# Attention with a feed-forward layer: another order of the first two chunks, with fixed buffer rooms

## The chip, the core and the metric

The kernel runs on one core of one Trainium2 chip. TensorE (PE in the rows) multiplies matrices, VectorE (DVE), ScalarE (ACT) and GpSimd (POOL) work on vectors, and SyncE (SP) issues the DMAs. Each engine takes its instructions strictly in the order of the program and waits on semaphores for the others. The metric is the device time of one execution in microseconds (us).

## What is computed

Local attention with block summaries over 4 batches, 8 heads, 768 positions and 64 features a head, and then a two-layer feed-forward network on its output. Everything is float32.

```python
k_sum = k.reshape(B, H, nb, block, D).max(axis=3)      # 24 blocks of 32
v_sum = v.reshape(B, H, nb, block, D).mean(axis=3)
scores_l = where(|i - j| < 16, scale * q @ k.T, -1e9)   # scale 1/8
scores_s = scale * q @ k_sum.T + log(32)
a = softmax(concat([scores_l, scores_s]))
x = a @ concat([v, v_sum])                              # 3072 x 512
h = maximum(x @ w_in, 0)                                # 512 -> 2048
out = (h * h) @ w_out                                   # 2048 -> 512
```

## The kernel before

**Tiling.** Of the 3072 rows, 128 make a group (24 groups, 6 a batch) and two groups a chunk of 256 (12 chunks). The 2048 hidden features are 16 tiles of 128. A weight arrives as the words of a float64 and is made on the chip into a high and a low float32r half; each product of the feed-forward layers is then three matmuls (high times high, low times high, high times low). One feature tile of a chunk costs 12 matmuls of 256 columns in the first layer (`ffn1`, L382) and 6 of 512 columns, some of them halved, in the second (`ffn2`, L429).

**Two parts.** The chunks 2 to 11 run in a regular loop (`slot`, `period`) that the change does not touch. The first two chunks (groups 0 to 3), the whole preparation of the weights, and the attention of groups 4 to 7 are written out by hand in one string, `START` (L43). Each of its tokens is one step, and the steps are emitted in the order of the string, so the string sets the order on each engine. The framework adds the waits for the data and for buffers that are used again. The tokens are:

- `L:..` a load on SP: `q`, `k`, `v` of a group, `kv` and `kw` (transposed keys of batch 0, keys and values of batch 1, a head pair each), `w` (the words of a feature tile: `w2.1` the half for the first layer, `w2.2` for the second, `w4` both), `vn` (values of batch 0), `mask` (constants).
- `KS` block maxima of a pair's keys (DVE, L180); `S4.0` half the scores of group 4 (PE, L285 for groups 0 to 3, L269 later); `TT0.3` mask and maximum of group 0, head 3 (DVE, L297); `E0.3` its exponential (ACT, L305); `NR` and `N` reciprocal sums (DVE, L318) and the normalisation (POOL, L325) of four heads.
- `T` a transposition on PE (L331) and `TC` its copy out of PSUM (L126). `SV` block means of the values on PE (L149) and `VC` four copies of them, two instructions each, into the two value buffers. `O` the attention output (PE, L352), `XH` and `XL` its high and low half (ACT L366, DVE L369).
- `HI`, `LO`, `SH`, `AD`, `CA`, `SU` the six steps that make a weight (ACT; ACT or DVE; DVE; POOL; ACT or DVE; DVE or POOL).
- `F1.u.j` and `F2.u.j` first and second layer of unit `u`, a pair of feature tiles of chunk 0 or 1; `RE`, `SQ`, `MU`, `GL` the square of its result. `Z15` fifteen matmuls of zeros that fill PE. `XT` one small exponential. A letter `a`, `v` or `p` behind a token names the engine; digits behind `=` name PSUM banks.

**Buffers.** Weights, raw words and key/value tiles share one pool of 18 buffers of 8 KB a partition (`room`, L209), given out in turn. A load waits until the buffer's last use is over, and DMAs wait in SP's queue in order. At most eight DMAs of SP are under way, since eight semaphores are used in turn.

Of the kernel before, what the change touches and what calls it, by code (L numbers as in the profile page):

```python
# [40 lines left out]


START = """  # L43
Z15 XT L:q0 L:kv0 L:kv1 KS0 L:kv3 KS1 L:kv2 KS3 S0.0=01 Z6 L:mask KS2 TT0.3 S0.1=23 TT0.1 L:q1 TT0.0 L:w0.1 L:w1.1
TT0.2 S1.0=45 L:q2 TT0.6 E0.3 TT0.4 E0.1 L:w2.1 TT0.7 S1.1=45 Z5 E0.0 E0.6 PK4v E0.2 NR0.0 TT1.7 TT1.0 TT1.2 E0.4
HI0.1 E1.7 L:q3 TT1.5 TT1.1 TT1.3 E1.2 LO0.1v N0.0p SH0.1 T0.0=0 Z2 HI1.1 E1.1 TT0.5 TT1.6 E1.3 S2.1=12 SH1.1 LO1.1v
S2.0=12 E1.0 TC0.0v TT1.4 E0.7 NR1.0 TT2.0 E1.5 TT2.3 E0.5 S3.1=30 AD1.1 S3.0=30 E1.4 E1.6 NR1.1 N1.0p HI2.1 E2.3
CA1.1v TT2.1 N1.1p E2.0 CA0.1a T1.0=4 Z2 NR0.1 TT3.2 TT3.0 L:vn0 L:vn1 L:q4 T1.1=5 Z1 TT3.1 TC1.0v L:k4 E3.1 N0.1p
E3.2 SU1.1p L:v1 T0.1=4 TT3.4 TT3.7 TT3.6 SV Z1 TT3.5 E3.0 TT3.3 TC1.1a E3.3 AD0.1 E2.1 TT2.7 SU0.1p TT2.4 L:v0 TT2.5
TC0.1a TT2.2 E2.7 E3.6 S4.1=03 TT2.6 NR3.0 N3.0p E2.2 S4.0=03 L:w3.1 VC1v E2.5 E3.4 E2.6 E3.5 VC0v VC3v L:w0.2 VC2v  # L50
NR2.0 L:w1.2 PK5v SH2.1 E2.4 E3.7 O1=5 N2.0p NR2.1 O0=1 XH1 XH0 HI3.1 NR3.1 XL1 T2.0=2 N3.1p LO2.1a T3.0=4 CA2.1a XL0
TT4.2 HI0.2 TC3.0v TT4.0 L:v3 T3.1=5 LO3.1a TC2.0v N2.1p TC3.1a AD2.1 LO0.2v F1.0.0=1 L:v2 T2.1=4 TC2.1a F1.0.1 O3=2
O2=5 SH3.1 CA3.1a HI1.2 SH0.2 SU2.1v XH3 L:w2.2 L:w3.2 AD3.1 CA0.2a L:q5 RE0v XH2 LO2.2a F1.1.0=4 SU3.1v SH1.2 F1.1.1
HI3.2 HI2.2 SQ0 L:w4 XL3 RE1a TT4.6 AD0.2 L:w6 LO1.2v XL2 SH2.2 L:k5 F1.2.0=2 SH3.2 MU0 LO3.2a MU1 AD1.2 TT4.7
F1.3.0=5 L:w5 GL0v SU0.2v F1.2.1 CA1.2a L:kw0 HI4 SQ1 LO4a L:w8 L:w7 SH4 F2.0.0 L:w10 CA2.2v SU1.2v CA3.2a AD2.2
SU2.2v AD3.2 RE2v TT4.4 GL1v HI6 TT4.1 F1.3.1 F2.0.1 CA4a TT4.5 L:w12 S5.1=14 SU3.2p S5.0=14 MU2 F2.1.0 E4.4 LO6a RE3v
AD4 HI5 SQ2 F2.1.1 SH6 TT4.3 SU4v E4.2 SH5 EV0.1a SQ3 F1.4.0=0 AD6 CA6a MU3 L:w9 L:w11 F1.6.0=3 GL2v EV0.0v SU6v TT5.0
TT5.1 LO5a F2.2.0 GL3v TT5.5 HI8 F1.5.0=2 CA5a F2.2.1 HI7 AD5 TT5.4 LO7v SU5v F1.7.0=5 SH8 LO8a SH7 HI10 TT5.2 F1.4.1
L:kw1 RE4v TT5.3 TT5.7 CA7a MU4 SH10 AD7 F1.6.1 LO10a E4.7 L:q7 SU7v F2.3.0 F2.3.1 SQ4 CA8a GL4v F1.5.1 HI12 AD8 RE6v
RE5v AD10 F2.4.0 MU5 F2.4.1 SQ5 CA10a HI9 F1.7.1 SH12 GL5v SU8p LO12a TT5.6 MU6 RE7a CA12a SH9 L:w13 SU10v SQ6 LO9a  # L60
VT1 AD12 F2.5.0 MU7 SU12v F2.5.1 L:w14 EV1.0a L:q6 SQ7 EV1.1v GL6v F1.8.0=0 KT1 CA9a HI13 F1.13.0=2 L:w15 L:k7 GL7p
KT0 F1.12.0=1 AD9 F1.10.0=4 E4.5 L:v5 LO13v SU9v HI11 F2.6.0 E5.7 F2.6.1 SH13 SH11 F1.9.0=5 E4.1 VT0 E4.3 E5.1 E4.0
F1.8.1 L:k6 CA13a E5.6 F2.7.0 CA11a E5.4 HI14 AD13 LO11v SU13v RE8v SQ8 E5.0 L:v4 AD11 NR4.0 E5.5 F2.7.1 MU8 SU11v
F1.14.0=3 E4.6 SH14 F1.10.1 CA14a GL8v E5.3 RE10a F1.12.1 NR5.1 F1.9.1 N4.0p LO14v F1.13.1 RE9v AD14 F2.8.0 F1.14.1
NR4.1 SQ9 MU9 F2.8.1 MU10 HI15 GL9v F2.9.0 LO15a SQ10 SH15 SU14v N4.1p AD15 E5.2 F1.11.0=0 TU4.1 F2.9.1 GL10v CA15a
TU4.2 TU4.0 RE12v F2.10.0 SU15p L:kw2 KT2 F1.11.1 RE11a NR5.0 L:kw3 SQ11 F1.15.0=5 MU11 GL11v RE13a F2.10.1 N5.1v KT3
F2.11.0 SQ12 MU12 N5.0p MU13 F2.11.1 PK6a GL12p F1.15.1 SQ13 EV2.1v S6.1=01 S6.0=01 O4=4 EV2.0v PK7a F2.12.0 F2.12.1
GL13p TU5.0 F2.13.0 RE14a TU5.2 XH4 SQ14 MU14 RE15a F2.13.1 GL14p TU5.1 VT2 S7.0=23 XL4 SQ15 S7.1=23 F2.14.0 MU15
GL15v O5=4 VT3 F2.14.1 XH5 XL5
"""  # L70


# [1 line left out]
def attn_ffn_kernel(ctx: ExitStack, tc: tile.TileContext, q, k, kt, v, vt, v0, w, consts, out):  # L74
    nc = tc.nc
# [63 lines left out]
    def load_v(g):  # L139
        nc.sync.dma_start(out=v_sb[g % 2][0:96], in_=v[g // NT, g % NT])  # L140

    def sum_v0(vn):
# [10 lines left out]
        return ps
# [583 lines left out]
```

## Time and profile before

| what | before |
|---|---|
| median of 3 runs | 606.64 us (606.45 to 610.62) |
| the profiled execution | 607.6 us, its span 605.8 us |
| TensorE busy | 593.8 us, 98% of the span |
| VectorE, ScalarE, GpSimd busy | 386.0, 265.8, 105.2 us |
| TensorE clock granted | 0.999 on the mean, that is the 2.4 GHz level |
| last wait of TensorE for another engine or a DMA of the kernel | 36.7 us after the span's start |

The span runs from the first instruction to the last. The 1.8 us between it and the execution's time lie around it. The share of busy time is a mean over two very different parts, so stretches of it are shown further down.

### The profile page before, as it was taken

The page shows a single profiled execution, that of the slowest core. Times are in us where ns is not written, and L with a number is a line of the kernel's source. Part 1 is how long each engine was busy: PE and PEld are TensorE (multiplying, and loading weights), DVE is VectorE, ACT ScalarE, POOL GpSimd, SP SyncE. Part 2 cuts the span into 40 slices and gives each one's busy share as a digit, 9 for nine tenths or more (in the row PEclk, how much of TensorE's full clock was granted, in tenths as well). Part 3 has the DMA queues.
Part 4 walks back from the last instruction along what each step waited for, and adds up shares of the span by engine and source line. Part 5 has one row for each costly group of instructions (what it writes and reads, how often), then busy time and mean ns, then how long its engine had stood idle before and what let it go on. Part 6 is the DMA issues. An engine that isn't in the chain of part 4 may idle for free.

```text
span 605.8 us, 14834 instructions
## 1 busy us (share of the span) xinstructions
PE 593.8 (98%) x6178; PEld 572.8 (95%) x6178; DVE 386.0 (64%) x1063; ACT 265.8 (44%) x687; POOL 105.2 (17%) x97
## 2 busy tenths in 40 slices
...
GB/s 274 328 363 417 204 260 56 112 168 35 1 11 269 2 2 226 2 2 226 2 1 199 81 2 131 97 2 87 88 2 38 139 2 2 88 1 2 36 1 35
DMA packets 19890, 60.46 MB, mean 100 GB/s; under 512 B 2288, under 2 KB 2288, under 8 KB 18288
## 3 DMA queue, kind: packets, MB, share of 16 engines
...
## 4 chain that ended last, share of the span: by engine, by line
PE 95%; DMA 3%; DVE 1%; ACT 0%; issue 0%; SPq 0%
PE o_ps L429 43%; PE ph L382 39%; PE s_ps L382 4%; PE ph L352 4%; PE s_ps L269 3%; DMA v_sb<-in_v 1%; DMA q_sb<-in_q 1%; DMA kv<-in_kt 1%; DVE v_sb L126 1%; PE s_ps L285 0%; PE o_ps L149 0%; PE o_ps L563 0%; PE ph L331 0%; PE ph L285 0%; PE s_ps L352 0%
## 5 line engine op out<-in xcount | busy, mean ns | idle before, releaser
L382 PE MATMUL ph<-xh,w_sb 128*128 128x256 f32 x1376 | 241.2, 278 | 0.5 <-DVE xl L369 0.5
L429 PE MATMUL o_ps<-w_sb,gh 128*128 128x256 f32 (+1 forms) x1428 | 237.5, 285 | 0.0
L382 PEld LDWEIGHTS ph<-xh,w_sb 128*128 128x128 f32 x1376 | 213.3, 188 | 8.7 <-issue 1.3
L429 PEld LDWEIGHTS o_ps<-w_sb,gh 128*128 128x128 f32 x1428 | 191.0, 188 | 0.5 <-issue 0.3
L382 PE MATMUL ph<-xl,w_sb 128*128 128x256 f32 x688 | 190.5, 277 | 0.0
L429 PE MATMUL o_ps<-w_sb,gl 128*128 128x256 f32 (+1 forms) x670 | 150.5, 294 | 0.0
L401 DVE TENSOR_TENSOR ph<-ph,r 128x512 f32<-128x512 f32 x85 | 59.3, 699 | 141.5 <-ACT r L390 140.7
L390 ACT ACTIVATE r<-ph 128x512 f32<-128x512 f32 x84 | 49.9, 594 | 189.3 <-PE ph L382 189.3
L382 PEld LDWEIGHTS ph<-xl,w_sb 128*128 128x128 f32 x688 | 129.2, 188 | 0.0
L338 DVE STREAM_TRANSPOSE pT<-e_sb 32x256 f32<-32x256 f32 x240 | 104.6, 436 | 4.1 <-POOL e_sb L325 0.7
L305 ACT ACTIVATE e_sb<-e_sb,nmx 128x120 f32<-128x120 f32 x192 | 73.7, 386 | 75.5 <-DVE nmx L297 75.5
L429 PEld LDWEIGHTS o_ps<-w_sb,gl 128*128 128x128 f32 x670 | 104.6, 188 | 0.4
L325 POOL TENSOR_TENSOR e_sb<-e_sb,total 128x480 f32<-128x480 f32 x47 | 46.2, 991 | 322.1 <-DVE total L319 150.4
L396 ACT ACTIVATE gh<-r 128x512 fp32r<-128x512 f32 x94 | 59.5, 633 | 12.1 <-PE o_ps L429 6.5
L404 DVE TENSOR_TENSOR gl<-ph,gh 128x512 fp32r<-128x512 f32 x85 | 58.8, 692 | 9.2 <-DVE ph L401 0.5
L297 DVE CUSTOM_DVE_ANT_0 e_sb<-s_ps,consts_sb 128x120 f32<-128x120 f32 x180 | 40.7, 277 | 1.9 <-PE ph L331 1.1
L245 POOL TENSOR_TENSOR w_raw<-w_raw 128x1024 int32<-128x1024 int32 (+1 forms) x20 | 35.9, 1800 | 24.7 <-DVE w_raw L234 8.6
L305 ACT ACTIVATION_READ_ACCUMULATOR e_sb<-e_sb,nmx 128x1 f32 x192 | 36.3, 189 | 0.0
L369 DVE TENSOR_TENSOR xl<-ph,xh 128x512 fp32r<-128x512 f32 x22 | 15.2, 691 | 23.3 <-ACT xh L366 23.2
L382 PE MATMUL s_ps<-xh,w_sb 128*128 128x256 f32 x160 | 28.6, 279 | 0.0
L366 ACT CAST xh<-ph 128x512 fp32r<-128x512 f32 x22 | 12.9, 586 | 33.1 <-PE ph L352 33.1
L352 PEld LDWEIGHTS ph<-pT,v_sb 128*64 128x64 f32 x704 | 21.7, 138 | 5.2 <-issue 3.8
...
## 6 DMA issues: line engine op xcount, KB each, us to landing
...
```

The source lines that it names most:

```text
L245: nc.gpsimd.tensor_tensor(out=lo, in0=hi, in1=lo, op=ALU.add)
L297: nc.vector.tensor_tensor_reduce(out=e_sb(g)[:, h, 0:NK], in0=s_ps[g, half][h % 2][:, h // 2, 0:NK], in1=m, scale=-scale, scalar=3.0e38, o ...
L305: nc.scalar.activation(e, e, AF.Exp, bias=nmx[g, half][:, i : i + 1], scale=-1.0, accum_out=sm[g, half][:, i, 0:1])
L325: eng.tensor_mul(out=e, in0=e, in1=sm.pop((g, half)).unsqueeze(2).to_broadcast([P, 4, NK]))
L338: nc.vector.transpose(out=pT[g % 2][j * 32 : j * 32 + 32, :, i * 32 : i * 32 + 32], in_=e_sb(g)[i * 32 : i * 32 + 32, :, j * 32 : j * 32 + ...
L352: nc.tensor.matmul(xp[o : o + 64, h // 2, s * 64 : s * 64 + 64], lhsT=v_sb[g % 2][:, s, h * 64 : h * 64 + 64], rhs=pT[g % 2][:, h, s * 64 ...
L382: nc.tensor.matmul(ph, lhsT=w_sb[f][:, w, cc * P : (cc + 1) * P], rhs=x[c][:, cc, :], start=(n == 0), stop=(n == 3 * NC4 - 1))
L390: nc.scalar.activation(r, ph, AF.Relu)
L396: nc.scalar.activation(gh, r, AF.Square)
L401: nc.vector.tensor_mul(out=ph, in0=ph, in1=r)
L404: nc.vector.tensor_sub(out=gl, in0=ph, in1=gh.bitcast(F32))
L429: nc.tensor.matmul(o_ps[c][tt][:, o : o + step], lhsT=g_[:, ts_], rhs=w_sb[f][:, w, DM + o : DM + o + step], start=start and o == 0, stop= ...
```

## The change

The string `START` is written anew: 508 tokens for 506, nearly the same steps in another order, some of them on another engine. The buffers of the pool are no longer given out in turn; each tile has a fixed room, from tables. The load of the constants is split in two (the masks that the first groups use, and the rest), and the block means of the values are split in two halves. The loop behind the string is the same, instruction for instruction. Line numbers behind the tables are 2 to 4 higher after the change.

```diff
 SPARE = 2
+RAW_ROOM = (5, 3, 2, 10, 12, 14, 15, 16, 8, 3, 5, 0, 8, 14, 3, 0)
+W_ROOM = (7, 9, 4, 11, 13, 1, 17, 10, 2, 15, 16, 6, 12, 8, 5, 14)
+KV0_ROOM, VN_ROOM, KV_FIRST, KV_ROOM = (0, 1), (6, 8), (3, 12, 5, 6), (0, 3)
...
-Z15 XT L:q0 L:kv0 L:kv1 KS0 L:kv3 KS1 L:kv2 KS3 S0.0=01 Z6 L:mask KS2 TT0.3 S0.1=23 TT0.1 L:q1 TT0.0 L:w0.1 L:w1.1
...
+L:kv1 KS1 L:q0 L:kv0 Z15 KS0 S0.0=01 L:mask TT0.1 TT0.0 TT0.2 E0.2 TT0.3 E0.3 L:q1 S1.0=45 E0.0 TT1.1 E1.1 TT1.0 E1.0
+Z6 L:kv2 KS2 L:kv3 KS3 L:w2.1 E0.1 S0.1=23 S1.1=45 TT0.5 TT1.2 HI2.1 E0.5 LO2.1v NR0.0 N0.0p E1.2 L:rest TT1.5 TT1.3
...
-    def sum_v0(vn):
...
-        ps = ps_o.tile([P, DM], F32, name="o_ps")
-        for t in range(NT):
+    def sum_v0(vn, n, ps):
+        if n == 0:
+            ps = ps_o.tile([P, DM], F32, name="o_ps")
+        for t in range(n * NT // 2, (n + 1) * NT // 2):
...
-    def room(dtype, name):
...
-        return big.tile([P, 8192 // mybir.dt.size(dtype)], dtype, name=name, tag="w", bufs=NF + SPARE)
+    def room(dtype, name, n):
...
+        return big.tile([P, 8192 // mybir.dt.size(dtype)], dtype, name=name, tag=f"room{n}")
...
-            w_raw[f] = room(I64, "w_raw")
+            w_raw[f] = room(I64, "w_raw", RAW_ROOM[f])
...
-            nc.sync.dma_start(out=consts_sb, in_=consts)
+            nc.sync.dma_start(out=consts_sb[:, 0 : 2 * NK], in_=consts[:, 0 : 2 * NK])
+        elif what == "rest":
+            nc.sync.dma_start(out=consts_sb[:, 2 * NK :], in_=consts[:, 2 * NK :])
...
-            v_mean[0] = sum_v0([vn[0], vn[1]])
+            v_mean[0] = sum_v0(vn, i, v_mean.get(0))
```

Three places of the order follow. Numbers behind `e_sb`, `pT` and `v_sb` tell apart the buffers of even and odd groups.

ScalarE, the start of the program before, with the semaphores that each row waits for: `XT` (`junk`) comes first, then exponentials of group 0.

```order
L640 ACT_TABLE_LOAD
L640 ACTIVATE junk<-zero_90 128x1 [waits DVE_49]
L305 ACTIVATE e_sb_77,sm<-e_sb_77,nmx 128x120 [waits DVE_49] x4
L305 ACTIVATE e_sb_77,sm<-e_sb_77,nmx 128x120
L305 ACTIVATE e_sb_77,sm<-e_sb_77,nmx 128x120 [waits DVE_49]
```

And ScalarE, the same place after the change:

```order
L307 ACT_TABLE_LOAD [waits DVE_49]
L307 ACTIVATE e_sb_77,sm<-e_sb_77,nmx 128x120 [waits Pool_49]
L307 ACTIVATE e_sb_77,sm<-e_sb_77,nmx 128x120 [waits DVE_49]
L307 ACTIVATE e_sb_77,sm<-e_sb_77,nmx 128x120
L307 ACTIVATE e_sb_78,sm<-e_sb_78,nmx 128x120 [waits DVE_49] x2
```

`XT` has moved to some 100 rows further down, and the table load now stands behind the first exponential's wait for VectorE.

ScalarE, after the change, around the output of groups 0 and 1. Before, the eight copies into `v_sb` stood on VectorE, and all 32 exponentials of groups 0 to 3 stood ahead of the first `xh`.

```order
L129 CAST w_sb<-w_raw 128x512
L307 ACTIVATE e_sb_78,sm<-e_sb_78,nmx 128x120 x2
L129 COPY v_sb_73<-o_ps 32x2x128
L129 COPY v_sb_74<-o_ps 32x2x128
L129 COPY v_sb_73<-o_ps 32x2x128
L129 COPY v_sb_74<-o_ps 32x2x128
L307 ACTIVATE e_sb_77,sm<-e_sb_77,nmx 128x120 x2
L307 ACTIVATE e_sb_78,sm<-e_sb_78,nmx 128x120
L368 CAST xh<-ph 128x4x128
L307 ACTIVATE e_sb_78,sm<-e_sb_78,nmx 128x120
L307 ACTIVATE e_sb_77,sm<-e_sb_77,nmx 128x120
L368 CAST xh<-s_ps 128x4x128
```

Four of the copies came to ScalarE, and three exponentials moved behind the second `xh`.

TensorE before, from the zeros behind the block means to the first matmuls of the first layer (`xh,w_sb`): scores of group 4, outputs of groups 1 and 0, three transpositions.

```order
L563 MATMUL o_ps<-zero 128x512
L269 MATMUL s_ps<-k_sb_71,q_sb_75 64x120 x16
L352 MATMUL ph<-pT_80,v_sb_74 64x64 x16
L352 MATMUL s_ps<-pT_79,v_sb_73 64x64 x16
L331 MATMUL s_ps<-consts_sb,e_sb_77 128x128 x4
L331 MATMUL ph<-consts_sb,e_sb_78 128x128 x8
L382 MATMUL s_ps<-xh,w_sb 128x256 x2
```

TensorE after, the same place:

```order
L567 MATMUL o_ps<-zero 128x512 x3
L354 MATMUL ph<-pT_80,v_sb_74 64x64 x16
L354 MATMUL s_ps<-pT_79,v_sb_73 64x64 x16
L333 MATMUL ph<-consts_sb,e_sb_78 128x128 x4
L567 MATMUL o_ps<-zero 128x512
L333 MATMUL s_ps<-consts_sb,e_sb_77 128x128 x4
L384 MATMUL s_ps<-xh,w_sb 128x256 x2
```

The scores of group 4 and one transposition of group 3 now stand behind the first two tiles of the first layer.

## Rows read from the trace of the kernel before

**Rows 1.** The page: busy us, share of the span, instructions of TensorE and the others.

```profile
PE 593.8 (98%) x6178; PEld 572.8 (95%) x6178; DVE 386.0 (64%) x1063; ACT 265.8 (44%) x687; POOL 105.2 (17%) x97
```

**Rows 2.** Windows: stretch and its length, busy us (instructions) by engine, clock, DMA.

```profile
45.00:60.00 15.00, 15.00 (x144) 14.13 (x143) 14.59 (x32) 13.01 (x19) 8.06 (x4) 1.00 1.02 417
```

**Rows 3.** Groups by line, TensorE, first 38 us: busy us, mean ns, idle before.

```profile
L563 PE MATMUL o_ps<-zero 128*128 128x512 f32 x32 | 10.2, 452 | 1.2 <-DVE zero L116 1.2
```

**Rows 4.** Timeline of ScalarE: start, us, line, operation, [idle before <-releaser].

```profile
0.73 1.28 ACT L640 ACT_TABLE_LOAD   x1 [0.73 <-PEq L727]
2.02 0.20 ACT L640 ACTIVATE junk<-zero 128x1 f32<-128x1 f32 x1
10.38 0.40 ACT L305 ACTIVATE e_sb<-e_sb,nmx 128x120 f32<-128x120 f32 x1 [8.15 <-DVE nmx L297]
...
10.78 0.38 ACT L305 ACTIVATE e_sb<-e_sb,nmx 128x120 f32<-128x120 f32 x1
...
11.16 0.38 ACT L305 ACTIVATE e_sb<-e_sb,nmx 128x120 f32<-128x120 f32 x1
...
21.96 0.56 ACT L126 COPY pT<-ph 128x512 f32<-128x512 f32 x1
...
28.41 0.58 ACT L366 CAST xh<-ph 128x512 fp32r<-128x512 f32 x1 [1.24 <-PE ph L352]
29.47 0.59 ACT L366 CAST xh<-s_ps 128x512 fp32r<-128x512 f32 x1 [0.47 <-PE s_ps L352]
29.95 0.70 ACT L229 ACTIVATE w_raw<-w_raw 128x512 f32<-128x512 f32 x1
30.54 0.65 ACT L236 ACTIVATE w_raw<-w_raw 128x512 int32<-128x512 uint32 x1
```

**Rows 5.** Timeline of VectorE, the same columns.

```profile
7.25 2.90 DVE L180 TENSOR_REDUCE ksum<-kv 128x24 f32<-128x768 f32 x3 [1.86 <-DMA kv<-in_kt]
10.07 0.27 DVE L297 CUSTOM_DVE_ANT_0 e_sb<-s_ps,consts_sb 128x120 f32<-128x120 f32 x1
...
24.29 3.10 DVE L126 COPY v_sb<-o_ps 32x256 f32<-32x256 f32 x8 [0.69 <-PE o_ps L149]
...
30.09 0.69 DVE L369 TENSOR_TENSOR xl<-s_ps,xh 128x512 fp32r<-128x512 f32 x1 [0.37 <-ACT xh L366]
```

**Rows 6.** Timeline of TensorE, the same columns.

```profile
19.30 0.66 PE L331 MATMUL ph<-consts_sb,e_sb 128*128 128x128 f32 x4
19.71 0.68 PE L563 MATMUL o_ps<-zero 128*128 128x512 f32 x2
...
25.21 1.05 PE L269 MATMUL s_ps<-k_sb,q_sb 64*64 64x120 f32 x32 [0.54 <-DMA k_sb<-in_k]
...
30.83 0.50 PE L382 MATMUL s_ps<-xh,w_sb 128*128 128x256 f32 x2
...
33.59 0.33 PE L331 MATMUL ph<-consts_sb,e_sb 128*128 128x128 f32 x1 [0.78 <-issue]
...
36.72 1.15 PE L352 MATMUL ph<-pT,v_sb 128*64 128x64 f32 x32 [0.20 <-DMA v_sb<-in_v]
```

**Rows 7.** DMA issues of the first 4 us: tile, KB each, median us to landing.

```profile
consts_sb<-in_consts SPq DMA_DIRECT2D x1, 270.0 KB, 6.8
```

**Rows 8.** Timeline of VectorE and of GpSimd, steps of whole weight tiles.

```profile
43.77 0.70 DVE L240 TENSOR_SCALAR w_raw<-w_raw 128x1024 int32<-128x1024 int32 x1
...
49.86 1.21 DVE L254 TENSOR_TENSOR w_sb<-w_raw,w_sb 128x1024 fp32r<-128x1024 f32 x1
51.00 2.38 DVE L240 TENSOR_SCALAR w_raw<-w_raw 128x1024 int32<-128x1024 int32 x1
...
49.88 2.95 POOL L245 TENSOR_TENSOR w_raw<-w_raw 128x1024 int32<-128x1024 int32 x1 [0.69 <-DVE w_raw L240]
```

**Rows 9.** Chain of work that ended last: start, us, what.

```profile
37.88 3.02 PE ph L382 x24
...
53.32 2.74 PE s_ps L382 x24
```

More of the change, by code (lines that the diff above doesn't have):

```diff
@@ L43 @@
 START = """
-Z15 XT L:q0 L:kv0 L:kv1 KS0 L:kv3 KS1 L:kv2 KS3 S0.0=01 Z6 L:mask KS2 TT0.3 S0.1=23 TT0.1 L:q1 TT0.0 L:w0.1 L:w1.1
[L45 to L68, printed above, removed]
@@ L69 @@
-GL15v O5=4 VT3 F2.14.1 XH5 XL5
+L:kv1 KS1 L:q0 L:kv0 Z15 KS0 S0.0=01 L:mask TT0.1 TT0.0 TT0.2 E0.2 TT0.3 E0.3 L:q1 S1.0=45 E0.0 TT1.1 E1.1 TT1.0 E1.0
+Z6 L:kv2 KS2 L:kv3 KS3 L:w2.1 E0.1 S0.1=23 S1.1=45 TT0.5 TT1.2 HI2.1 E0.5 LO2.1v NR0.0 N0.0p E1.2 L:rest TT1.5 TT1.3
+E1.3 TT0.7 SH2.1 NR1.0 Z5 N1.0p Z2 L:w1.1 HI1.1 L:q2 S2.0=12 E0.7 SH1.1 E1.5 CA2.1a TT0.4 E0.4 TT1.6 E1.6 TT0.6
+S2.1=12 T0.0=0 TT1.4 T1.0=4 E1.4 TT2.3 TT2.2 E0.6 TC0.0a E2.2 TT1.7 L:q3 S3.1=30 AD2.1 SU2.1p E1.7 L:w0.1 LO0.1a NR0.1
@@ new lines @@
+TC1.0v S3.0=30 NR1.1 N0.1p TT2.0 T0.1=4 TT3.0 E3.0 TT3.1 TT2.1 TC0.1v L:vn0 TT2.6 E3.1 E2.3 TT3.3 TT2.5 HI0.1 SH0.1
+TT3.2 N1.1p T1.1=5 TC1.1a E3.3 E3.2 TT3.7 CA0.1a SV0 L:vn1 TT2.4 TT3.5 AD0.1 SV1 TT3.4 E3.4 PK4v E3.7 LO1.1v AD1.1
+VC2a L:v1 VC1a E2.1 NR3.0 VC0v E2.0 E3.5 VC3v Z2 Z1 TT3.6 O1=5 XH1 E3.6 L:v0 O0=1 SU0.1p TT2.7 E2.7 N3.0p T3.0=4 NR2.0
+N2.0p XL1 CA1.1v SU1.1p Z1 T2.0=2 NR3.1 N3.1p XH0 XL0 L:w3.1 F1.0.0=1 E2.5 E2.6 E2.4 NR2.1 TC3.0v L:w1.2 LO1.2a TC2.0v
+HI1.2 SH1.2 L:q4 L:w3.2 LO3.1v HI3.2 HI3.1 LO3.2a SH3.1 F1.0.1 RE0v N2.1p T2.1=4 TC2.1a L:k4 T3.1=5 TC3.1a S4.0=03
@@ new lines @@
+TT4.1 S4.1=03 TT4.6 PK5v TT4.0 CA3.1v SH3.2 CA3.2a TT4.2 F1.1.0=4 L:v3 O3=2 TT4.3 XH3 E4.2 AD3.1 L:v2 O2=5 XH2 SU3.1p
+F1.1.1 L:w0.2 MU0 CA1.2a XL3 HI0.2 L:w2.2 HI2.2 TT4.5 AD3.2 AD1.2 XL2 SU1.2v F1.3.0=5 SU3.2v SH0.2 RE1v LO0.2a TT4.4
+SQ0 CA0.2a L:w4 SH2.2 SQ1 CA2.2v F1.3.1 E4.5 AD0.2 SU0.2v GL0v LO2.2a AD2.2 E4.4 MU1 HI4 SH4 F1.2.0=2 F1.2.1 LO4a
+SU2.2v AD4 F2.0.0 CA4a F2.0.1 GL1v L:q5 L:k5 S5.0=14 S5.1=14 RE2v TT4.7 L:w5 HI5 MU2 TT5.1 SQ2 LO5a SH5 AD5 TT5.7 L:w6
+HI6 F2.1.0 F2.1.1 EV0.1a SU4v F1.4.0=0 GL2v RE3a TT5.5 EV0.0v L:w7 HI7 F2.2.0 F2.2.1 SH6 CA6a E4.1 SQ3 CA5v SU5v LO6a
@@ L70 @@
+F2.12.1 RE14a SQ14 XH4 XL4 MU14 F1.15.1 GL13p RE15v PK7a GL14p F2.13.0 F2.13.1 SQ15 S7.1=23 S6.0=01 S6.1=01 S7.0=23
+MU15 VT0 O5=4 XH5 F2.14.0 F2.14.1 GL15v XL5
 """
@@ L167, in load_kv0 @@
         if (p // 2) not in padded:
-            padded[p // 2] = r = room(F32, "kv")[:, 0 : 2 * KPAD].rearrange("p (a k) -> p a k", a=2)
+            padded[p // 2] = r = room(F32, "kv", KV0_ROOM[p // 2])[:, 0 : 2 * KPAD].rearrange("p (a k) -> p a k", a=2)
             nc.gpsimd.memset(r[:, :, 0:WINDOW], 0.0)
@@ L174, in load_kv @@
     def load_kv(b, p):
-        kv[b, p] = r = room(F32, "kv")
+        kv[b, p] = r = room(F32, "kv", KV_FIRST[p] if b == 1 else KV_ROOM[p % 2])
         nc.sync.dma_start(out=r[:, 0:S], in_=kt[b, p])
```

14 lines of the change are left out of this document (12 added, 2 removed).

## The prediction

> **What bounds the kernel now.** The page gives TensorE 593.8 us of a span of 605.8 us [rows 1], so it sits idle for 12.0 us in all. The granted clock is full, 2.4 GHz, in the stretch shown [rows 2]. Next I asked where the idle time lies. The window from 45 to 60 us has TensorE busy for 15.00 of 15.00 us, with the other three engines nearly full beside it [rows 2], and the last wait in its timeline is 0.20 us before 36.72 us, for a load of values [rows 6]. So from there on the kernel is TensorE's own work, and the change, which leaves that work as it is, can only move the start of this dense stretch or tear a hole into it. Before 38 us TensorE also runs 32 matmuls of zeros, 10.2 us of them [rows 3], which fill waits. Idle time and zeros together, some 22 us, are the most that any order could win, and loads and arithmetic ahead of the first product take most of that.
>
> The yardstick is a fixed set of work: the scores of groups 0 to 4, all transpositions and outputs of groups 0 to 3, and F1.0.0, F1.0.1 and F1.1.0. Before, F1.1.0 follows the last output in the chain at 37.88 us. It and its neighbour take 3.02 us for 24 matmuls [rows 9], 1.51 us each, so the set is done at 39.4 us. What follows is dense, so each microsecond by which the set ends earlier or later is one of the result, as long as no new wait comes behind it.
>
> Ahead of it ScalarE sets the pace: it runs 32 exponentials in a row, from the first at 10.38 us to the `xh` casts at 28.41 and 29.47 us, with idle times of 1.24 and 0.47 us before these two [rows 4]. The first of them waits for the block means, copied by VectorE in 3.10 us [rows 5].
>
> **The change, part by part.**
>
> *First exponential.* Before, the last block maximum ends at 10.1 us and masks start at 10.07 us [rows 5]. The constants are issued sixth and take 6.8 us to land [rows 7], which is just ahead of that. After, the first three loads are the same bytes (two key pairs and `q`), so the second key pair is there at 7.2 us as now [rows 5]. One maximum takes 2.90/3 = 0.97 us. The rest of half a group's scores takes about 0.5 us (a whole group takes 1.05 us [rows 6]) and the way to VectorE 0.2 us, so masks start at 8.9 us. The smaller constants come fourth and are no longer waited for. E0.2 needs the third mask, so it is ready near 9.7 us. This is a gain of 0.7 us, but the table load of 1.28 us, which runs at 0.73 us now while nothing is ready [rows 4], stands behind that wait after the change. First exponential: 9.7 + 1.3 = 11.0 us, 0.6 us later than now. Its old cover was ScalarE's empty start; here it has none.
>
> The Trainium skill says in "ScalarE: Activation LUTs", section "What ACT_TABLE_LOAD costs", that a switch of sets costs some 1283 ns and a DRAIN of some 1380 ns more. The trace agrees on the load. It shows no drain after it, since `junk` starts at 2.02 us, 0.01 us after the load [rows 4]. With the drain the sum would be 1.4 us higher; this is a rival below.
>
> *ScalarE to the second `xh`.* After, 29 exponentials at 0.38 us (10.78 to 11.16) make 11.0 us, six steps of weight halves at 0.57 us (29.95 to 30.54, less a little) 3.4 us, two copies `TC` at 0.46 us (0.56 us less the overlap of 0.1 that the casts show) 0.9 us, the first `xh` 0.48 us and the second 0.59 us [rows 4]. New are four of the eight copies into `v_sb`. No row has them on ScalarE. Below, half of `TC` each for half its columns, 0.9 us together; above, VectorE's 0.39 us each (3.10/8), 1.6 us [rows 5]. I take 1.2 us, as a fixed part is likely. Sum: 17.6 us. Waits that I find by following the lists: E3.0 needs scores that write the PSUM bank which `TC0.0` frees late (0.4 us); SH1.1 meets a normalisation on GpSimd and delays a mask (0.3 us); the outputs come a little after ScalarE is ready (0.2 us). End: 11.0 + 17.6 + 0.9 = 29.5 us against 29.47 + 0.59 = 30.06 us. So the old idle times and the three exponentials that are put off pay for the table load and the copies. With `xl` (0.69 us [rows 5]) and the small gaps of now (30.09 to 30.83), F1.0.0 starts at 30.3 us, 0.5 us earlier.
>
> *From F1.0.0 to the end of the set.* Before: 30.83 to 39.4 us, 8.6 us, of which 0.78 us (issue) and 0.20 us (values) are waits [rows 6]; I put the smaller gaps beside them at 0.4 us. That leaves 7.2 us of work. After, the scores of group 4 (1.05 us) and one transposition (0.41 us, 19.30 to 19.71 [rows 6]) are still to do: 8.7 us. The issue wait has no cover that I could name: between 0 and 0.78 us, I take 0.2 us, since only one stretch of the start shows it in this size. End: 30.3 + 8.7 + 0.2 = 39.2 us, a gain of 0.2 us. The last output needs values that land at 36.7 us now [rows 6]. The outputs that free their buffer come about 1 us earlier in my sums, and with F1.1.0 ahead the values are wanted only at 37 us.
>
> *Behind the set.* The fixed rooms cost nothing by themselves: I followed each, and what a load or a cast waits for there has been done some microseconds before. The tightest spot is tile 4. Before, its last step SU4 ends at 51.07 us [rows 8], and F1.4.0 starts at 53.32 us [rows 9]: 2.2 us to spare. After, SU4 stands behind a mask of group 5, whose scores end some 2.8 us before F1.4.0 (four matmul stages, 3.02 us, less a little), and behind SH5 (0.70 us), two masks (0.4 us) and its own 1.21 us: about 0.4 us to spare. I take it at nothing.
>
> Sum: 0.2 us less. On the profiled execution 607.6 becomes 607.4 us (its span 605.8 becomes 605.6). The median of the three runs is 606.64 us, 1.0 us under that execution, so the forecast is 606.4 us.
>
> **The rivals.**
>
> *The start wins more.* If VectorE or the loads, not ScalarE, carry the first 30 us, the late table load falls into idle time and its 1.3 us come back, or the copies cost the lower bound and the issue wait does not recur (0.5 us together). For it: two idle times of 1.24 us stand in ScalarE's present chain. Against: after the change I find it waiting for under 1 us. Time: 606.4 - 1.8 = 604.6 us.
>
> *Slower: tile 4 comes too late.* SH of a whole tile takes 0.70 us alone and took 2.38 us while an addition on GpSimd held out for 2.95 us beside it [rows 8]. If SH5 meets such an addition (AD4), SU4 ends 1.7 us later, 1.3 us behind F1.4.0. It decides from a delay of 0.4 us on. For it: VectorE, ScalarE and GpSimd are busy for most of that stretch [rows 2]. Against: AD4 should be over before SH5 starts. Time: 606.4 + 1.3 = 607.7 us; with one more such meeting at the next tile, 609 us.
>
> *The list does nothing.* All that is won at the start is lost to the table load and a recurring issue wait: 606.4 + 0.6 = 607.0 us. It can't be told from my forecast by the time alone.
>
> *The table load drains.* If ScalarE stands still after the load as well, the whole chain moves. No row has such a stop. The nearest, the 0.01 us at 2.02 us, speaks against it, and the bound on the other side is a second load, 1.28 us [rows 4]: 607.7 us. By the skill's page it would be 607.8 us.
>
> **How the numbers follow.** About what a measurement of this kernel can tell from no change is 1%, 6 us. Forecast with its own range of 605.4 to 607.2 us, the do-nothing case included: 0.55. More won, 603.5 to 605.4 us: 0.17. Tile 4 late, 607.2 to 609 us: 0.16. Drain: 0.04. Something that I don't see, a load held up or a room in use, over 6 us: 0.06; a gain over 6 us, which needs over a quarter of the 22 us: 0.02. The range 604.3 to 608.3 us leaves out under 2 in 10. So faster by over 1% 0.02, within 1% 0.92, slower by over 1% 0.06.
>
> **What would show it.** The table load near 9.7 us, with the first exponential right behind it. The second `xh` ending near 29.5 us, F1.0.0 starting near 30.3 us. No wait of TensorE behind 39.2 us; one before F1.4.0, near 53 us, means that tile 4 was late. SH5 over 1 us long means a meeting with GpSimd. I am wrong if the table load runs at the start, if an idle time of over 1 us opens on ScalarE between 11 and 29 us, or if TensorE waits behind 60 us.

## The result, and the profile after

| what | before | after |
|---|---|---|
| median | 606.41 us (605.15 to 610.62, 20 runs) | 610.46 us (607.09 to 612.62, 20 runs) |
| after / before, 95% interval | | 1.0058 [1.0045, 1.0071] |
| the profiled execution, its span | 607.6, 605.8 us | 610.42, 608.6 us |
| TensorE busy | 593.8 us | 595.5 us |

The change makes the kernel 3.5 us (by the ratio) to 4 us (by the medians) slower. That is within the 1% that I gave 0.92, but outside the range of 604.3 to 608.3 us.

The page after, its first part: busy us of each engine, share of the span, instructions. TensorE's 6182 matmuls take 1.7 us more than in [rows 1], and the span is 2.8 us longer.

```profile
PE 595.5 (98%) x6182; PEld 574.0 (94%) x6182; DVE 384.1 (63%) x1058; ACT 268.2 (44%) x692; POOL 103.2 (17%) x97
```

Windows of after: stretch, length, then busy us (instructions) of TensorE, of its weight loads, of VectorE, ScalarE and GpSimd, then granted clock, DMA share, GB/s. The third row answers [rows 2]: behind 45 us TensorE is as full as it was, so the loss lies ahead.

```profile
15.00:30.00 15.00, 9.68 (x203) 7.03 (x195) 8.81 (x56) 11.56 (x46) 9.50 (x9) 0.89 0.98 291
30.00:45.00 15.00, 14.00 (x223) 12.72 (x220) 11.29 (x40) 10.48 (x27) 8.57 (x8) 1.00 0.99 339
45.00:60.00 15.00, 15.00 (x149) 14.37 (x148) 13.62 (x30) 13.52 (x21) 6.99 (x4) 1.00 1.01 417
...
24.00:26.00 2.00, 0.15 (x4) 0.15 (x8) 0.30 (x3) 0.57 (x4) 1.87 (x2) 0.91 1.03 238
26.00:28.00 2.00, 2.00 (x26) 1.46 (x23) 0.00 (x0) 0.58 (x2) 1.36 (x2) 0.50 1.02 249
```

The first row shows where: before, that window (below) has TensorE busy for 11.37 us at full clock, and VectorE for 11.95 us.

```profile
15.00:30.00 15.00, 11.37 (x295) 9.44 (x295) 11.95 (x66) 12.05 (x54) 10.54 (x10) 1.00 1.02 328
```

The last two rows of after narrow it down: in 24 to 26 us TensorE, VectorE and ScalarE are all nearly idle (0.15, 0.30 and 0.57 of 2.00 us), while the loads run, and in 26 to 28 us TensorE is granted 0.50 of its clock, the 1.2 GHz level.

The chain of after, in order of time (start, us, what), names what they wait for: one load of 11.86 us, the second half of the raw values (`vn`), from which the block means are made.

```profile
13.01 0.42 SPq L220
13.43 0.05 issue
13.48 0.42 SPq L549
13.95 11.86 DMA vn<-in_v
25.85 1.55 PE o_ps L151 x24
27.42 0.63 ACT v_sb L129 x2
28.06 0.64 ACT v_sb L129 x2
28.72 0.75 DVE v_sb L129 x2
29.50 0.79 DVE v_sb L129 x2
30.34 0.82 PE ph L354 x20
31.18 0.59 ACT xh L368
31.80 0.69 DVE xl L371
```

Timelines of after (start, us, engine, line, operation, [idle before <-releaser]). ScalarE first, which answers [rows 4]: the table load, the first exponential, the four copies of the means, the two `xh`.

```profile
8.96 1.28 ACT L307 ACT_TABLE_LOAD   x1 [8.96 <-DVE nmx L299]
10.26 0.40 ACT L307 ACTIVATE e_sb<-e_sb,nmx 128x120 f32<-128x120 f32 x1
...
27.42 1.27 ACT L129 COPY v_sb<-o_ps 32x256 f32<-32x256 f32 x4 [2.86 <-PE o_ps L151]
...
31.18 0.58 ACT L368 CAST xh<-ph 128x512 fp32r<-128x512 f32 x1 [1.22 <-PE ph L354]
...
32.44 0.57 ACT L368 CAST xh<-s_ps 128x512 fp32r<-128x512 f32 x1
```

VectorE, for [rows 5] and [rows 8]: its four copies start 0.03 us behind ScalarE's last, after an idle time of 4.39 us. SH5, further down, takes 0.70 us.

```profile
28.72 1.56 DVE L129 COPY v_sb<-o_ps 32x256 f32<-32x256 f32 x4 [4.39 <-ACT v_sb L129]
...
33.04 0.69 DVE L371 TENSOR_TENSOR xl<-s_ps,xh 128x512 fp32r<-128x512 f32 x1
...
49.93 0.70 DVE L242 TENSOR_SCALAR w_raw<-w_raw 128x1024 int32<-128x1024 int32 x1 [0.26 <-ACT w_raw L231]
```

TensorE, for [rows 6] and [rows 9]: the two halves of the means, each behind its load, the outputs, F1.0.0, the scores of group 4, F1.1.0, the last two outputs.

```profile
22.33 0.86 PE L151 MATMUL o_ps<-vn,consts_sb 128*32 128x128 f32 x24 [0.82 <-DMA vn<-in_v]
25.85 1.51 PE L151 MATMUL o_ps<-vn,consts_sb 128*32 128x128 f32 x24 [2.66 <-DMA vn<-in_v]
...
30.34 0.80 PE L354 MATMUL ph<-pT,v_sb 128*64 128x64 f32 x20 [0.19 <-DVE v_sb L129]
...
33.78 0.50 PE L384 MATMUL s_ps<-xh,w_sb 128*128 128x256 f32 x2 [0.47 <-DVE xl L371]
...
38.76 0.63 PE L271 MATMUL s_ps<-k_sb,q_sb 64*64 64x120 f32 x14 [0.34 <-DVE nmx L299]
39.33 0.51 PE L384 MATMUL ph<-xh,w_sb 128*128 128x256 f32 x2
...
41.89 1.10 PE L354 MATMUL ph<-pT,v_sb 128*64 128x64 f32 x32
42.93 0.50 PE L384 MATMUL ph<-xh,w_sb 128*128 128x256 f32 x2
```

Before, the means ran at one stretch with no wait ahead of them. This is its row:

```profile
21.99 1.51 PE L149 MATMUL o_ps<-vn,consts_sb 128*32 128x128 f32 x46
```

So F1.0.0 starts at 33.78 us instead of 30.83, and the yardstick set ends at 42.9 us instead of 39.4. Behind it TensorE waits no more than before: once, for 0.48 us near 550 us, in both traces.

### The profile page after: what moved, and what is told of

It is laid out like the page before. It is cut to its first block, busy times and chain, and to the rows that moved or that the text cites. A ratio compares the mean times of both kernels' runs of the same rounds, so it can differ in the third digit from the quotient of the medians.

```text
span 608.6 us, 14849 instructions
## 1 busy us (share of the span) xinstructions
PE 595.5 (98%) x6182; PEld 574.0 (94%) x6182; DVE 384.1 (63%) x1058; ACT 268.2 (44%) x692; POOL 103.2 (17%) x97
## 4 chain that ended last, share of the span: by engine, by line
PE 94%; DMA 3%; DVE 1%; ACT 0%; SPq 0%; issue 0%; DVEq 0%
PE o_ps L431 43%; PE ph L384 39%; PE s_ps L384 5%; PE ph L354 3%; PE s_ps L271 3%; DMA vn<-in_v 2%; DMA q_sb<-in_q 1%; DVE xl L371 0%; DVE ksum L182 0%; PE o_ps L151 0%; DVE v_sb L129 0%; PE ph L287 0%; ACT v_sb L129 0%; ACT xh L368 0%; PE s_ps L354 0%
## 5 line engine op out<-in xcount | busy, mean ns | idle before, releaser
L247 POOL TENSOR_TENSOR w_raw<-w_raw 128x1024 int32<-128x1024 int32 (+1 forms) x20 | 34.1, 1709 | 28.2 <-ACT w_raw L238 12.2
L384 PEld LDWEIGHTS s_ps<-xh,w_sb 128*128 128x128 f32 x160 | 24.8, 188 | 1.4 <-DVE xl L371 0.7
```

Of the source, the lines that this page charges most:

```text
L247: nc.gpsimd.tensor_tensor(out=lo, in0=hi, in1=lo, op=ALU.add)
L384: nc.tensor.matmul(ph, lhsT=w_sb[f][:, w, cc * P : (cc + 1) * P], rhs=x[c][:, cc, :], start=(n == 0), stop=(n == 3 * NC4 - 1))
```

## The experiments

Seventeen runs follow, most of them of after with a few tokens moved, one of before as it is. The diffs show pieces of lines of `START`. "Span" is that of the profiled execution. A landing is the trace's time at which a load was complete.

**Is it the table load?** `XT` goes back to the front.

```diff
-L:kv1 KS1 L:q0
+XT L:kv1 KS1 L:q0
```

> The changed kernel with XT back at the front of the list, so that the table load runs at 0.7 us again. Theory of the late values (the second half of the batch-0 values, vn1, lands at 25.8 us, and the block means, the copies into v_sb and the outputs wait for it): ScalarE gets to its exponentials 1.3 us earlier and waits 1.3 us longer for the block means; vn1 still lands near 26 us, the time stays at 610.4 us within 0.7. Theory of the table (my forecast's term: the load stands on the path): 1.3 us less, 609.1 us.

610.55 us, 1.0056 [1.0034, 1.0078]: no gain. The first exponential came at 9.18 us, 1.08 us earlier than in after, but ScalarE reached the copies only 0.2 us earlier (24.36 against 24.56 us; a wait of 0.51 us for a mask had opened on the way). There it waited 2.87 us, as in after, since the values landed at 25.61 us. While the values are as late as that, the table load does not count.

**Is it the values?** Two other orders of the loads.

```diff
-L:q2
+L:vn0 L:q2
-L:q3
+L:q3 L:vn1
```

> The changed kernel with vn0 issued ahead of q2 and vn1 right behind q3, ahead of w0.1, so that SP's wait for the scores of groups 0 and 1 does not hold vn0. Theory of the late values: vn1 lands at 18 to 20 us, the block means follow the transpositions near 21.5 us without a wait, F1.0.0 starts near 30 us in place of 33.8, the granted clock stays at 1.0, time 605.5 to 607.5 us. Theory of the table: the path is ScalarE's from the start, time 609.5 us or more.

611.82 us, 1.0082 [1.0052, 1.0112]: slower still, though `vn1` landed at 18.75 us and no mean waited. Now `q2` landed at 16.21 us instead of 14.62, groups 2 and 3 came 1.6 us later, and F1.0.0 started at 33.38 us. The wait had only moved to another load.

```diff
-L:v1 VC1a
+L:w3.1 L:w1.2 L:v1 VC1a
```

> The changed kernel with the loads w3.1 and w1.2 moved ahead of v1 and v0, so that 1024 KB stand between vn1 and the loads of 96 partitions. If the v loads in flight beside it slow vn1 down: vn1 lands at 22.5 to 23.5 us, TensorE's wait before the second half of the block means shrinks from 2.7 us to under 1 us, time 607 to 609 us. If vn1 is late by its place in the queue alone: it lands at 25.8 us as before the move and the time stays at 610.4 us.

610.84 us, 1.0074 [1.0045, 1.0103]. `vn1` landed at 24.49 us, 1.3 us earlier, but `v1` only at 30.70 us, and the outputs waited 3.21 us for that.

**Is it the clock?** Zeros fill TensorE's waits around the means.

```diff
-SV0 L:vn1
+Z3 SV0 Z11 L:vn1
```

> The changed kernel with 3 matmuls of zeros ahead of the first half of the block means and 11 between the halves, where TensorE stands idle for 0.8 and 2.7 us. vn1 lands as late as before (near 26 us). Theory of the clock (the idle time lets TensorE's granted clock fall to 1.2 GHz, and the work behind runs slowly): the mean clock is 0.999 or more in every run, time 607 to 608.5 us, the level of those runs of the changed kernel whose clock was 1.0. If the late load costs all of it and the clock nothing: 610.4 us.

610.24 us, 1.0056 [1.0032, 1.0080]. The window shows what they did: from 24 to 26 us TensorE is busy throughout at clock 1.00.

```profile
24.00:26.00 2.00, 2.00 (x31) 1.38 (x30) 0.00 (x0) 0.20 (x3) 2.00 (x2) 1.00 1.02 242
```

All eight executions had a mean clock of 0.997 or more, and none was faster than 608.62 us. So a kept clock alone does not bring the time back. The zeros cost here, too: in the traced execution `vn1` landed at 23.55 us and the second half of the means started at 25.06, when the last zero was done.

**Is it the split of the copies?** ScalarE writes one of the two buffers, VectorE the other.

```diff
-    def place_v0(ps, j, eng):
-        for g in range(2):
+    def place_v0(ps, n, eng):
+        g = 1 if n in (1, 2) else 0
+        for j in ((0, 1) if n in (0, 2) else (2, 3)):
```

> After, with the eight copies of the means shared out by buffer instead of by columns: ScalarE makes the four of one buffer of v_sb, VectorE the four of the other, so that neither writes a tile that the other writes. The theory that the split copies ran one behind the other only because they wrote the same two tiles (ScalarE 27.42 to 28.69, VectorE 28.72 to 30.28 in after): VectorE starts when ScalarE does, the first outputs (O1) come at 29.0 instead of 30.34, F1.0.0 at 32.5 instead of 33.78, and the time is 609.2 us, 1.3 below after's 610.5. The rival, that the two engines cannot read the sums in PSUM at the same time: VectorE still starts behind ScalarE or the copies get longer, and the time stays at 610.5. The theory that the clock is what costs: the idle TensorE between 22 and 27 stays, so the runs still scatter from 607 to 612 by their clock.

609.05 us, 1.0049 [1.0025, 1.0074], against after's 1.0058 [1.0045, 1.0071]: not to be told apart. The copies still ran one behind the other, although the two engines no longer wrote the same tile (VectorE's waits, us in total, times, longest):

```profile
DVE v_sb L129 <- ACT v_sb L129: 6.3, 1, 6.3
```

The wait is in the program. This is VectorE's first copy in the compiled list, in after as here:

```
L129 COPY v_sb_73<-o_ps 32x2x128 [waits PE_49,Activation_49]
```

What the two engines still share is the tile of PSUM that both read. The edit also makes each engine read all four strips of 32 partitions of that tile, where in after each reads two of its own. So the run does not tell which sharing the wait in after comes from. The traced execution was the slowest of its ten, 612.69 us, and its `vn1` landed at 28.02 us with the same order of loads as after.

**The weight behind the values.** `vn0` and `vn1` ahead of the half weight `w0.1`, whose steps move behind the copies.

```diff
-L:q3 S3.1=30
+L:q3 L:vn0 L:vn1 L:w0.1 S3.1=30
-VC3v Z2
+VC3v HI0.1 SH0.1 LO0.1a AD0.1 CA0.1a Z2
-XL1 CA1.1v
+XL1 SU0.1v CA1.1v
```

> After, with the two loads of the raw values issued ahead of the first tile's half weight (w0.1) but still behind q2 and q3, and the five steps on that half moved behind the copies of the means, its subtraction onto VectorE. Late values: w0.1 took 4.25 us of the queue between q3 (15.37) and vn0, so vn1 lands near 21.5 instead of 25.80 without delaying q2, TensorE's second sums start at 21.6, O1 comes near 26.5 and F1.0.0 near 30.8; the time is 607.0 us. The rival from the run with the early values (611.8 us), that other waits take over: then F1.0.0 comes at 32.5 or later although vn1 has landed before 22, held by the half weight that now comes last or by the copies, and the time is 609.5 or above. Clock: with the sums no longer waiting there is no fall, and the runs lie within 1.5 us of each other.

609.09 us, 1.0038 [1.0020, 1.0057], and all ten executions within 1.6 us of each other, near the 1.5 us expected for a start without the long wait. But the fall of the clock was expected to stay away: only the traced execution has a mean clock of 1.0, the other nine 0.996 or 0.997, as after's trace has with one fall of 3.4 us. `vn1` landed at 22.96 us, the copies ended at 26.78 us, but F1.0.0 came at 32.25 us: ScalarE made the weight ahead of `xh`.

**Put the late values into before.** The two loads behind `q4` and `k4`, in before's own list.

```diff
-L:vn0 L:vn1 L:q4 T1.1=5 Z1 TT3.1 TC1.0v L:k4
+L:q4 T1.1=5 Z1 TT3.1 TC1.0v L:k4 L:vn0 L:vn1
```

> Before, with one edit: the two loads of the raw values are issued behind q4 and k4 instead of ahead of them. They should land near 23 and 25 instead of 19.74 and 21.61. Late values as the cause: the sums end near 26.6 instead of 23.9, the eight copies on VectorE near 29.8, O1 at 29.9 instead of 27.44, F1.0.0 at 33.2 instead of 30.83, and before becomes 2.4 us slower, 608.8, or 610 to 611 if TensorE's clock falls in the wait as it did in after. If late values are not enough by themselves (the copies or the order of the steps are the cause), the time stays within 0.7 us of 606.4.

611.32 us, 1.0070 [1.0045, 1.0096]. `vn1` landed at 26.97 us, F1.0.0 came at 35.21 us, the mean clock fell to 0.989 to 0.994 in all ten. Late values, with nothing else of the change, cost before 4.6 us, the fall of the clock that came with them included.

**q4 ahead of v_sb.** The rate of the loads in after is about halved in 22 to 28 us (238 and 249 GB/s in the window rows above; 410 in 18 to 20 us). The two loads of `v_sb`, of 96 partitions, are under way then. Here they are issued at 18 us instead of 14.4.

```diff
-VC2a L:v1
+VC2a L:q4 L:v1
```

> After, with one load moved: q4, which waits for its buffer until about 17.6, is issued ahead of the two loads of v_sb, so these are issued after 17.6 instead of at 14.42 and 14.89, as before's list has them (18.10 and 18.58). The theory that the loads of 96 partitions, in flight since 14.4, are what halves the rate for the loads ahead of them: w0.1 lands near 17, vn0 near 19, vn1 near 21 to 22, O1 near 26.5, and the time is 607.0 to 607.8. The rival, that the rate falls for another reason: vn1 still lands at 24 or later and the time is 609.5 to 610.5.

609.26 us, 1.0043 [1.0014, 1.0071], with four of ten executions at 607.3 to 608.3 us, all of these at clock 1.0. In the traced one (608.28 us) `vn1` landed at 23.34 us and F1.0.0 started at 31.45 us.

**All together.** Values ahead of the weight, `q4` ahead of `v_sb`, `XT` in front, VectorE's copies first; then the same with after's copies.

```diff
-L:q3 S3.1=30
+L:q3 L:vn0 L:vn1 L:w0.1 L:q4 S3.1=30
-TT3.7 CA0.1a SV0
+TT3.7 LO0.1a HI0.1 SH0.1 AD0.1 SV0
-SV1 TT3.4 E3.4
+SV1 VC1v VC2v TT3.4 VC0a VC3a CA0.1a E3.4
```

> After with the three terms mended together: the two loads of the raw values directly behind q3, then w0.1 and q4 ahead of the two loads of v_sb (so that vn1 comes early and the loads of 96 partitions after it); the table load back at the front; and the copies by buffer, VectorE's four first, right behind the sums, ScalarE's four behind them. Theory that late values and the place of the copies are all there is: vn1 lands near 20.5, the sums end near 23.2 on TensorE, VectorE copies to 24.8, ScalarE to 26.1, F1.0.0 comes at 29.0 to 30.4 (before 30.83), and since the span went by 0.96 us for each us of F1.0.0 so far, the time is 604.3 to 606.0, at or under before's 606.4, with no fall of the clock. Rival, that this list carries another cost behind the start of the first layer: F1.0.0 comes ahead of 30.5 and the time is still over 607.

> The same, but with the eight copies shared out and placed as in after (ScalarE's four behind its exponentials, then VectorE's four). If the loads alone are the cause: within 0.5 us of the run with all three. If the place and order of the copies cost as well: they start on ScalarE near 24.5 to 25 as in the run with q4 ahead (25.09), VectorE ends near 27.3, F1.0.0 comes near 30.9, 0.9 to 1.5 us later than with all three, and the time is 606.5, about that of before.

612.30 us, 1.0096 [1.0072, 1.0119], and 610.10 us, 1.0069 [1.0044, 1.0094]: misses. `vn1` landed at 19.69 and 22.43 us, but F1.0.0 came at 34.81 and 35.10 us. ScalarE and VectorE take their instructions in order, and the steps on the half weight, which now landed at 22.66 and 24.35 us, stood ahead of the copies. In the second trace ScalarE waited 1.49 us for that load. In the first it had landed, and ScalarE came to its steps only at 24.17 us, behind exponentials of groups 2 and 3.

**The weight back ahead**, with `q4` and `XT` in front and VectorE's copies right behind the sums, half of them or all.

```diff
-LO1.1v AD1.1 VC2a L:v1 VC1a E2.1
+LO1.1v VC1v VC2v AD1.1 L:q4 L:v1 VC0a VC3a E2.1
```

```diff
-LO1.1v AD1.1 VC2a L:v1 VC1a E2.1
+LO1.1v VC1v VC2v VC0v VC3v AD1.1 L:q4 L:v1 E2.1
```

> After with q4 ahead of the two loads of v_sb (as in the run that had vn1 at 23.34 and F1.0.0 at 31.45), the table load back at the front, and the copies by buffer with VectorE's four first, as soon as the sums end, ScalarE's four at their place behind it. The weights stay ahead of the raw values, since the two runs that moved w0.1 back only moved the wait to its steps. If each us of F1.0.0 is a us of the end: vn1 near 23.3, VectorE copies from about 24.6 to 26.2, the first outputs start there instead of at 28.0, ScalarE copies to about 27.4, F1.0.0 near 30.3, 0.5 ahead of before, and the fast end of the runs at or under 606. Rival: the copies' place is worth nothing, because groups 2 and 3 (their exponentials, divisions and transposes, which stand ahead of F1.0.0 on TensorE) or the loads of v_sb hold F1.0.0 at 31 to 31.5: 607.3 to 608.3.

> The same, with all eight copies on VectorE behind the sums, as before has them, and none on ScalarE: 24.6 to 27.7. If sharing them out is worth what ScalarE takes over (1.27 against 1.55 us) and no more: F1.0.0 0.3 later than in the run with the copies shared out, 606.5. If VectorE's later maxima are held by the four more copies: F1.0.0 1 us or more later and 607.5.

610.48 us, 1.0057 [1.0036, 1.0078], and 610.12 us, 1.0044 [1.0025, 1.0064]. `vn1` landed at 25.47 and 23.37 us. In the second trace the outputs started at 25.91 us, earlier than in before, and F1.0.0 still came at 31.59 us: the transposition of group 3 ahead of it waited 0.73 us for GpSimd, and GpSimd had waited 2.69 us for a sum of VectorE, which stood behind all eight copies (24.35 to 27.92 us). In that trace the earlier copies held up VectorE's next steps, and no gain was left. In the first run the values came too late to tell.

**Which load makes the values late?** First `q4` and `k4` both ahead of `v_sb` in after; then `v_sb` directly behind the values in before; then before a second time.

```diff
-VC2a L:v1
+VC2a L:q4 L:k4 L:v1
```

```diff
-L:vn0 L:vn1 L:q4
+L:vn0 L:vn1 L:v1 L:v0 L:q4
```

> After, with q4 and k4 both issued ahead of the two loads of v_sb, as before's list has them. In after 240 of the 256 packets of the raw values had begun by 21.96, but from 21.1, when other DMA engines were on the loads of v_sb, the last ones took 400 to 650 ns instead of 234, and the last began at 24.34. Theory that the loads of 96 partitions slow the tail of whatever is still under way: with 640 KB between, fewer than 5 of the last 128 packets take over 320 ns, the last begins near 21.5, vn1 lands near 22.5, and the time is 607.0 to 608.5. Rival, that the tail is slow by chance or by the loads ahead: vn1 lands at 24 or later and the time stays at 610.

> Before, with one edit: the two loads of v_sb are issued directly behind the two of the raw values, ahead of q4 and k4, as after has them. If these loads slow the tail of the raw values, more than 10 of the last 128 packets take over 320 ns (before: none), vn1 lands 1.5 to 4 us later than 21.61, q4 and k4 come late for the scores of tile 4, and before becomes 1.5 to 4 us slower, 608 to 610.5. The rival, that the order of the loads behind the raw values does nothing to them: vn1 lands at 21.6 and the time is 606 to 607 (the scores of tile 4 stand ahead of the first outputs in this list, so up to 0.7 us may come from k4).

> Before itself, for a second trace: whether the landing of the raw values (21.61) and F1.0.0 (30.83) move from run to run as they do in after's list (vn1 at 23.55 to 28.02 in four kernels with after's order of loads). If the scatter belongs to after's order alone: vn1 within 0.7 us of 21.61, no slow packet among the last 128. If it is any kernel's: 23 or later is as likely here.

The first gave 610.72 us, 1.0072 [1.0048, 1.0097], `vn1` at 25.19 us: no cure. The second gave 608.40 us, 1.0038 [1.0016, 1.0059], with `vn1` at 21.09 us, no later than in before; its loss comes with `k4`, for which the scores of group 4 waited 1.81 us, with clock 0.50 from 25.4 us for 3.4 us, and again from 59.6 us. Together they speak against `v_sb` as the cause by itself. The second trace of before has `vn1` at 21.16 us, F1.0.0 at 30.75 us and a span of 604.4 us.

**The weight into the hole.** Around 12 us after's loads stand nearly still, since `q2` heads SyncE's queue and waits for its buffer. Here `w0.1` is issued ahead of it; then the same with `XT` in front and `q4` ahead of `v_sb`.

```diff
-L:q2 S2.0=12
+L:w0.1 L:q2 S2.0=12
```

> After, with one load moved: the half weight w0.1 is issued ahead of q2 instead of behind q3. In after the loads stand almost still around 12 us (20 KB in that us), because q2 waits at the head of SyncE's queue for the scores of the first groups and w0.1 and the raw values stand behind it; here w0.1 fills that hole. Theory that the half weight at that place is what makes the raw values late and lets the DMA engines drift apart: w0.1 lands near 14.5, q2 no later than 15.2, vn1 near 19.5 to 21 with few slow packets at its end, F1.0.0 at 31.0 to 31.5, the time 606.3 to 607.3 and no scatter by the clock. Rival, that the tail of the raw values is slow whatever stands ahead: vn1 at 23 or later, 609 to 610.5.

> The same, with the table load at the front and q4 ahead of the loads of v_sb. With the values in time, ScalarE's chain of exponentials should be next, and the table load's 1.07 us should now count: the copies on ScalarE near 24 instead of 25.09, F1.0.0 at 30.3 to 30.8, the time 605.7 to 606.4, at or just under before. Rival: the values are still late in most runs or groups 2 and 3 hold F1.0.0 at 31.5: 607.3 or above, no better than e16.

611.61 us, 1.0082 [1.0061, 1.0103], and 609.88 us, 1.0070 [1.0049, 1.0091]: misses again. `vn1` landed at 23.02 and 25.26 us, and `q2` at 15.66 and 15.84 us, 1 us later than in after, for which TensorE idled and lost its clock at 17 us.

**What holds over all of them.** The traced executions, with after's list behind the front in all but the first two rows:

| kernel | `vn1` landed | F1.0.0 | span |
|---|---|---|---|
| before | 21.61 | 30.83 | 605.8 |
| before again | 21.16 | 30.75 | 604.4 |
| q4 ahead of v_sb | 23.34 | 31.45 | 606.5 |
| the same, copies on VectorE | 23.37 | 31.59 | 606.4 |
| vn ahead of w0.1 | 22.96 | 32.25 | 607.0 |
| zeros | 23.55 | 32.35 | 607.5 |
| w0.1 ahead, XT, q4 | 25.26 | 33.21 | 607.8 |
| values early | 18.75 | 33.38 | 608.3 |
| after | 25.80 | 33.78 | 608.6 |
| q4, XT, copies by buffer | 25.47 | 34.35 | 609.2 |
| XT first | 25.61 | 34.71 | 609.6 |
| all together | 19.69 | 34.81 | 610.8 |
| q4 and k4 ahead | 25.19 | 34.89 | 609.6 |
| w0.1 ahead of q2 | 23.02 | 34.98 | 610.0 |
| the loads only | 22.43 | 35.10 | 610.0 |
| weights ahead of v_sb | 24.49 | 35.85 | 610.6 |
| copies by buffer | 28.02 | 36.12 | 610.9 |

A line through the fifteen kernels with after's list (from the third row on) has a slope of 1.01: a microsecond of F1.0.0 is one of the span, whatever caused it. All lie within 0.4 us of it but one, "all together", where the clock was 0.50 while F1.0.0 ran. By that line after's list at before's 30.83 us would have a span of 605.7 us, that of the profiled before and 1.3 us over the second trace of before: the scores of group 4 and a transposition (1.05 and 0.41 us [rows 6]) still stand behind F1.0.0 in after's list. The two edited versions of before are not on this line: with late values F1.0.0 came at 35.21 us and the span was 608.3 us, with `v_sb` directly behind the values 31.72 and 609.0 us, the second fall of the clock behind F1.0.0 included. No version beats before, and by the intervals none of the versions of after is clearly faster than after; the nearest is `vn` ahead of `w0.1`.

## Why the prediction was wrong

**The yardstick held, nearly.** F1.0.0 was late by 2.95 us, the set by 3.5, and the span was longer by 2.8 us. The other 0.7 us came back behind the set; where was not followed. From F1.0.0 to the end of the set I had 8.9 us, and it took 9.1 (33.78 to 42.93). That nothing behind the set would wait is right as well: 15.00 of 15.00 us, SH5 at 0.70 us without a meeting with GpSimd, tile 4 in time. So the rival "tile 4 too late" fell.

**First exponential: 11.0 us predicted, 10.26 measured.** The table load does stand behind the wait for VectorE, and runs from 8.96 to 10.24 us, 0.7 us earlier than I had it, because the second key pair landed at 6.38 us. I counted its 1.28 us on the path. With it back at the front the time did not move (610.55 us). ScalarE did not stand still behind the load, as the rival had it: the exponential starts 0.02 us after it. So that rival fell. The Trainium skill's 1380 ns for a drain ("ScalarE: Activation LUTs", "What ACT_TABLE_LOAD costs") does not show behind this load; ahead of it ScalarE was idle, so one there could not be seen.

**ScalarE to the second `xh`: 29.5 us predicted, 33.0 measured. This step failed.** It was a sum of ScalarE's work with 0.9 us of waits. The work came out at 18.2 us, where I had 17.6. The waits were 0.46 (for `w0.1`), 2.86 (for the means) and 1.22 us (for the outputs), 4.5 us. The wait of 2.86 us is the sign of being wrong that the prediction named, an idle time of over 1 us on ScalarE between 11 and 29 us. I took the means as ready when ScalarE got to them, and never priced the load behind them: no term of the sum is `vn`. In the trace of before it lands at 21.61 us, just ahead of its use, with the means starting at 21.99 us. In after, as in before, both halves are issued behind `q2`, which now gets its buffer 1.15 us later than in before (12.04 against 10.89 us), since the first masks now run ahead of two block maxima on VectorE. At the landing of `vn1` the difference is 4.2 us; what made it grow is open (below). The chances had no place for such a loss: "a load held up" stood at 0.06 and for more than 6 us, and between 609 and 612.4 us there was nothing. That late values suffice is shown (before with late values: 611.32 us). That they are not the only thing at the limit is shown too: with values at 18.75 or 19.69 us another load or a weight's steps held F1.0.0 just as long.

**The copies: 1.2 us on ScalarE beside VectorE's predicted, 1.27 and then 1.56 us measured.** ScalarE's price was right. That the two parts overlap was assumed and wrong: 2.86 us from the first to the last against 3.10 us in one piece before, a gain of 0.24 us. A wait of VectorE for ScalarE's semaphore stood in the compiled list, where I could have read it. The Trainium skill has a rule near this ("PSUM — Partial Sum Buffer", "PSUM bank collisions raise a hardware error"): two engines must not use one bank in the same 32 partitions at once, reads included. It does not ask for the wait in after, where the two engines read different strips of 32 partitions. In all traces with copies on both engines they take turns, so no run here shows two engines reading at once.

**No term of the prediction was for the clock.** TensorE waited 0.82 and 2.66 us for the two loads, with 0.86 us of work between them, and from 25.65 us, at the end of the second wait, was granted 1.2 GHz for 3.4 us. Over after's 20 executions the time goes with it: those with a mean clock of 1.0 took 607.1 to 609.0 us, the nine at 0.991 or 0.992 took 610.6 to 612.6. How much of that is the clock and how much the later values that make TensorE idle, these runs don't separate; the run with zeros says that the clock is not all.

**The issue wait** of 0.78 us ahead of a transposition [rows 6], of which I counted 0.58 us as gained, was an accident of one execution: the second trace of before doesn't have it.

**Still open** is why the landing of `vn1` runs from 23.3 to 28.0 us in the nine traces that issue it behind `q3` and `w0.1`, as after does, and is 21.1 to 21.6 us in the three traces with before's front. In after 240 of the 256 packets of 6 KB of both halves had started by 21.96 us, at 234 ns each for the most part. The last sixteen took 380 to 580 ns and started one behind the other until 24.34 us, while packets of the next loads already ran beside them. The trace has sixteen updates of a load's semaphore, and the load has landed with the last. Those of `vn1` came between 20.36 and 21.61 us in before and between 20.81 and 25.80 us in after; with `w0.1` ahead of `q2`, `XT` and `q4`, fifteen had come by 20.24 us and the last one at 25.26. So a few parts of the load lag; what makes them lag is not shown.
